# Two schemes for the same seven products become one: both halves of a feed-forward block chained in three PSUM accumulators, with a set's third product issued behind the next set's first

## The chip, the cores and the metric

The kernel runs on one core of a Trainium2 chip. The metric is device time in microseconds of one execution. The engines are named as in the profile: PE is TensorE (with PEld for its weight loads), DVE is VectorE, ACT is ScalarE, POOL is GpSimd, SP is SyncE, which here only issues DMAs.

## The reference, cut to what matters

A transformer block on x of 2048 x 576 in fp32: a conditioned layer norm, attention with a compressive memory, a second conditioned layer norm, and a SwiGLU feed-forward block of width 4608. The change is in the last part alone:

```python
def _B_ref(x, w_gate, w_up, w_down):
    g = _silu(x @ w_gate)
    u = x @ w_up
    return (g * u) @ w_down
...
h = _layernorm(x, axis=-1) * (1 + cb) + sb
x = x + gb * _B_ref(h, B_w_gate, B_w_up, B_w_down)
```

## The kernel before, in words

The first third of the span is attention and its output projection, with the layer norms. The rest is the feed-forward block, in two halves of 1024 tokens (t = 0 and 1). Each half runs over 18 pairs p of 128-column strips of the 4608 columns. For a pair, a gate set (z = 0) and an up set (z = 1) of products are computed, then the products with w_down of the pair before are added to the outputs.

Every set is a fast 2 x 2 block matrix product (Winograd's form of Strassen): seven products m = 1 to 7 instead of eight. Each product is one function call, `prod` (L1139): seven matmuls of 512 columns, since the operands are split in a high and a low part (wh and wl for weights, y for the activations) with the last rows, wr, packed into one matmul of their own. The four results of a set are, by the products' numbers and with U = 1 + 6, V = U + 7: (0,0) = 1 + 2, (0,1) = U + 5 + 3, (1,0) = V + 4 and (1,1) = V + 5. `fin` (L1154) finishes a result: Silu for the gate, the product with the gate's result for the up set.

The two halves compute these sums differently.

- First half, `step0` (L1178): each product has a PSUM bank of its own (tag M, four buffers). ScalarE copies product 1 to SBUF (L1184); VectorE adds every later product to a running sum in SBUF (L1189, L1192) or in `fin` (L1160, L1168).
- Second half, `step` (L1199): products 1, 6, 7 and 4 accumulate on each other in bank A (two buffers); ScalarE copies A out behind product 1 (into bank B, onto which product 2 then accumulates, L1212), behind product 6 (tb) and behind product 7 (tc, both L1174). Products 5 and 3 accumulate in bank C. VectorE adds only for (1,1) and (0,1). In its very first set bank B has not been written yet, and product 1 goes to SBUF (cu).

The order of the work is written out by hand. A pair has 14 steps k, one product each, in an order from a table: `MO0` (1, 2, 6, 7, 4, 5, 3) for both sets in the first half, with the two sets of its last pair interleaved (`ZML`); `MO7` (1, 5, 6, 2, 7, 4, 3) in the second, `MOB` for its first set. Around each product a step issues, by its number k, casts of weights PF or PF0 products ahead (`prep_w`, ScalarE, with the low part on VectorE one step later through the list `later`), loads of weights (`load_o`, SyncE), sums of weights for the fast product (`sum_o`, GpSimd; in the first half only, stored by `store_o` and `store_r` through ScalarE's DMA queue, and loaded again in the second), casts of the results (`prep_a`) and of w_down (`prep_d`). The down-products of the pair before follow the product of the step: in the first half `plain` (L1276, eight chunks of 12 matmuls with 288 columns, at steps 4 to 11), in the second `down` (L1261, a fast product again, 14 chunks of six matmuls, by the table `CH`; its operands are sums of the results, `sum_a` at steps `KS` and casts at `KA`). The last two pairs of the second half use `plain` as well, at the steps of `CH0`. Down-products have a PSUM tag of their own (dn, two buffers of two banks), and VectorE adds each chunk to an accumulator in SBUF.

While the first half runs, `prep2` (L996) prepares the second half's input piece by piece (a generator, advanced at steps 1 to 10): it loads rows of x, normalizes, stores, loads them back as xb, transposes on TensorE into an M bank, scales on ScalarE, and forms the seven activation operands on GpSimd, which are stored as yD. At the end of the first half `load_y` (L1067) loads them over the first half's y, each as soon as its last product has run.

```python
A: [1] -> copy to B -> [1+6] -> copy tb -> [1+6+7] -> copy tc -> [1+6+7+4]
B: copy of 1, then + 2            C: 5, read for (1,1), then + 3
```

## Time and profile before

| | before |
|---|---|
| median of three runs | 1987.38 us (1987.2 to 1988.35) |
| the profiled execution | 1991.21 us |
| its span, first to last instruction | 1989.4 us |
| granted TensorE clock, mean | 0.986 |
| TensorE / VectorE / ScalarE / GpSimd busy | 96% / 80% / 45% / 29% |
| first half of the feed-forward block, first product to first product of the second | 662.48 to 1351.13 us |

The span is cut into 40 slices of 49.7 us in the second part of the page; a digit is the busy share in tenths. Slices 14 to 27 are the first half of the block, the rest the second. A line of a group of instructions gives source line, engine, operation, output <- inputs, shapes and count, then busy us and mean ns, then the idle time of the engine just before them and what ended it. A line of waits gives who waited for whom, us in total, how often, and the longest. M, A, B, C and pd are PSUM tiles, sg, cu, tb and tc are SBUF tiles.

### The profile page before, as it was taken

What the parts mean: (1) busy time and instruction counts of PE and PEld (TensorE: products, weight loads), DVE (VectorE), ACT (ScalarE), POOL (GpSimd) and SP (SyncE); (2) the same over time, 40 slices, a digit from 0 to 9 for tenths busy, and PEclk for the clock granted to TensorE, in tenths of its full rate; (3) what the DMA queues carried; (4) which work ended last, traced back from release to release, by engine and by line L of the source; (5) the groups of instructions that cost most, each with busy time, mean ns of one, the idle gap of its engine ahead of it and who ended that gap; (6) DMA issues with size and microseconds to landing.
All of it is one profiled execution on the core that took longest, in us unless ns stands there. A gap on an engine that the chain in (4) does not pass through costs nothing.

```text
span 1989.4 us, 30854 instructions
## 1 busy us (share of the span) xinstructions
PE 1904.3 (96%) x10927; PEld 1573.1 (79%) x10927; DVE 1598.7 (80%) x3411; ACT 894.3 (45%) x1928; POOL 583.4 (29%) x772
## 2 busy tenths in 40 slices
PE   7999999999998799999999998989999999999998
PEld 5888856676766678878888877878888888888888
DVE  6575257878786899999899999876888888888886
ACT  2222257767666333344334334333454544454542
POOL 5212235555535544544454444310000000000000
PEclk9999999999999899999999999999999999999999
DMA  7767564445435544444444544367333333232341
GB/s 212 242 225 238 205 190 127 141 137 149 132 111 145 193 162 158 166 163 143 149 153 161 174 130 148 114 216 246 129 98 118 99 98 118 79 120 90 118 120 48
DMA packets 173545, 296.64 MB, mean 149 GB/s; under 512 B 25104, under 2 KB 101776, under 8 KB 171920
## 3 DMA queue, kind: packets, MB, share of 16 engines
q1 hardware_dynamic: 145504, 239.79, 38.5%
q10 hardware_dynamic: 27888, 54.89, 7.6%
q8 instruction: 86, 1.41, 0.3%
q14 instruction: 67, 0.55, 0.1%
HBM read 185.29 MB, written 109.31 MB: 148 GB/s over the span
## 4 chain that ended last, share of the span: by engine, by line
PE 65%; DVE 22%; DMA 5%; issue 3%; ACT 3%; POOL 1%; ACTq 0%; SPq 0%; DVEq 0%; POOLq 0%
PE A L1146 12%; PE pd L1269 9%; PE C L1146 6%; PE pd L1286 6%; PE M L1146 5%; DVE wl L1111 4%; PE s L590 4%; PE av L610 4%; PE pp L102 4%; PE s L188 4%; PE B L1146 3%; PE pv L102 3%; PE pw L708 2%; DVE sg L1169 2%; DVE acc L1290 2%
## 5 line engine op out<-in xcount | busy, mean ns | idle before, releaser
L1146 PE MATMUL M<-y,wh 128*128 128x512 f32 x1008 | 364.0, 402 | 22.1 <-DVE cu L1168 14.8
L193 DVE CUSTOM_DVE_ANT_0 junk<-s,tri 128x256 bf16<-128x256 f32 (+3 forms) x512 | 228.8, 487 | 78.7 <-PE s L188 71.4
L1111 DVE TENSOR_TENSOR wl<-O,wh 128x256 fp32r<-128x256 f32 x504 | 269.4, 535 | 14.4 <-ACT wh L1110 13.8
L1146 PEld LDWEIGHTS M<-y,wh 128*128 128x128 f32 x1008 | 193.7, 192 | 71.9 <-issue 20.9
L1229 ACT CAST ah<-sg 128x512 fp32r<-128x512 f32 x192 | 118.9, 619 | 291.4 <-DVE sg L1169 244.1
L1101 POOL TENSOR_TENSOR O<-O 128x384 f32<-128x384 f32 x144 | 164.8, 1158 | 229.3 <-DMA O<-in_wgu_dram 120.7
L593 ACT ACTIVATE Pt<-s 128x512 f32<-128x512 f32 (+1 forms) x352 | 187.1, 560 | 87.8 <-PE s L590 73.8
L1110 ACT CAST wh<-O 128x256 fp32r<-128x256 f32 x504 | 200.0, 404 | 16.2 <-issue 12.3
L1146 PE MATMUL A<-y,wh 128*128 128x512 f32 x576 | 202.5, 392 | 0.7 <-ACT cu L1174 0.7
L1146 PE MATMUL M<-y,wl 128*128 128x512 f32 x504 | 201.5, 400 | 0.0
L1286 PE MATMUL pd<-dh,ah 128*128 128x288 f32 x640 | 190.0, 297 | 2.3 <-DVE acc L1290 2.3
L1286 PE MATMUL pd<-dh,al 128*128 128x288 f32 x640 | 189.5, 296 | 1.4 <-DVE al L1230 1.4
L1286 PE MATMUL pd<-dl,ah 128*128 128x288 f32 x640 | 189.3, 296 | 0.0
L1274 DVE TENSOR_TENSOR acc<-acc,pd 128x576 f32<-128x576 f32 x216 | 159.5, 751 | 24.9 <-PE pd L1269 23.1
L1230 DVE TENSOR_TENSOR al<-sg,ah 128x512 fp32r<-128x512 f32 x192 | 141.8, 739 | 21.2 <-ACT ah L1229 21.2
L590 PE MATMUL s<-qs,ks 110*128 110x512 f32 (+2 forms) x384 | 151.3, 411 | 5.3 <-DMA qs<-mD 3.5
L1161 ACT ACTIVATE sg<-sg 128x512 f32<-128x512 f32 x109 | 69.2, 635 | 183.6 <-DVE sg L1160 183.5
L1290 DVE TENSOR_TENSOR acc<-acc,pd 128x576 f32<-128x576 f32 x156 | 116.6, 748 | 38.5 <-PE pd L1286 38.0
L188 PE MATMUL s<-ks,qs 108*128 108x256 f32 (+3 forms) x512 | 142.3, 329 | 2.8 <-DMA ks<-kD 1.4
L1269 PE MATMUL pd<-dh,ah 128*128 128x288 f32 x448 | 132.8, 296 | 0.0
L1269 PE MATMUL pd<-dh,al 128*128 128x288 f32 x448 | 132.6, 296 | 0.0
L1269 PE MATMUL pd<-dl,ah 128*128 128x288 f32 x448 | 132.5, 296 | 0.0
(367 smaller groups left out, 4617.2 us busy)
## 6 DMA issues: line engine op xcount, KB each, us to landing
O<-in_wgu_dram SPq DMA_DIRECT2D x36, 768.0 KB
oD<-O ACTq DMA_DIRECT2D x36, 512.0 KB
O<-oD SPq DMA_DIRECT2D x36, 512.0 KB
ks<-kD SPq DMA_DIRECT2D x68, 216.0 KB
qs<-qD SPq DMA_DIRECT2D x68, 216.0 KB
O<-in_wgu_dram SPq DMA_DIRECT2D x36, 384.0 KB
rD<-wr ACTq DMA_DIRECT2D x36, 336.0 KB
wr<-rD SPq DMA_DIRECT2D x36, 336.0 KB
```

The source lines that it names most:

```text
L188: nc.tensor.matmul(bank[:, n * (h - h0):n * (h - h0) + n], lhsT=qst[b][0:108, h, 128 * i:128 * i + 128], rhs=kst[b][0:108, h // 2, 0:n], s ...
L193: nc.vector.tensor_tensor_reduce(junk[:, :n], bank[:, n * (h - h0):n * (h - h0) + n], tri[:, L - n:], 1.0, -3e38, op0=ALU.add, op1=ALU.max ...
L590: nc.tensor.matmul(bank[:, n * (g - h):n * (g - h + w)].rearrange("p (a b) -> p a b", a=w), lhsT=kst[u % NB][0:110, g // 2, 128 * j:128 * ...
L593: nc.scalar.activation(pt[:, h:h + per, :n], bank[:, :n * per].rearrange("p (a b) -> p a b", a=per), AF.Exp, scale=SCALE)
L1101: nc.gpsimd.tensor_tensor(o[:, d], o[:, a], o[:, b], op=op)
L1110: nc.scalar.copy(wh, o)
L1111: later.append(lambda: nc.vector.tensor_tensor(wl, o, f32(wh), op=ALU.subtract))
L1146: nc.tensor.matmul(bank, lhsT=a, rhs=b, start=(first and n == 0), stop=(n == 6), skip_group_check=not first)
L1269: nc.tensor.matmul(pd[:, i, :288], lhsT=a[:, tk], rhs=w, start=(k == 0), stop=(k == 2))
L1274: nc.vector.tensor_tensor(o, o, pd[:, :, :288], op=ALU.add)
L1286: nc.tensor.matmul(pd[:, i, :288], lhsT=a[:, tk], rhs=w, start=(k == 0), stop=(k == 5))
L1290: nc.vector.tensor_tensor(o, o, pd[:, :, :288], op=ALU.add)
```

## The change

`step0` and its orders go; both halves use `step`, and one loop over t and p takes the place of two. The order of a set is 1, 6, 2, 7, 5, 4, and product 3 of a set is issued behind product 1 of the next set: step 1 computes product 3 of the previous pair's up set, step 8 that of the pair's own gate set. Step 1 of the very first pair has no product, and one product 3 is left for the end, before the last down-products. A third result comes later by that: `prep_a` of (1,1) is at step 13, of (1,0) at step 0 and, in the plain case, of (0,1) at step 2 of the next pair. To match, the down-products of the fast kind come in another order (`POS`), with their sums and casts later (`KS`, `KA`), and the plain ones at steps 2 to 5 and 7 to 10 in both halves. Weight casts run five products ahead throughout. The transposes of `prep2` go to a buffer of the tag dn instead of M. The reloads of y are issued at steps 7 and 9 to 13 of the first half's last pair and at step 1 of the second half.

```diff
-PF0 = 6
-CH0 = (0, 1, 1, 0, 1, 1, 0, 1, 0, 1, 1, 1, 0, 0)
+CH0 = (0, 0, 1, 1, 1, 1, 0, 1, 1, 1, 1, 0, 0, 0)
-KS = (0, 1, 2, 3)
-KA = ((5, 2), (6, 4), (7, 6), (3, 8))
+KS = (2, 3, 4, 5)
+KA = ((5, 3), (6, 5), (7, 7), (3, 8))
-WW = (19, 23, 25, 26, 27, 30)
+WW = (19, 23, 25, 27, 30)
-    POS = [1, 2, 4, 5, 6, 7, 3]
+    POS = [1, 4, 2, 5, 6, 7, 3]
...
+    MP = (1, 6, 2, 7, 5, 4, 3)
+    ZM = [(z if m != 3 else 1 - z, m) for z in range(2) for m in (1, 3, 6, 2, 7, 5, 4)]
...
-                    pt = ps.tile([P, 4, P], F32, tag="M", name="pt", bufs=4)
+                    pt = ps.tile([P, 2, L], F32, tag="dn", name="pt", bufs=2)[:, 0].rearrange("p (a b) -> p a b", b=P)
...
-    def step0(p, z, m):
-        bank = ps.tile([P, L], F32, tag="M", name=f"M{m}", bufs=4)
-        prod(z, m, bank, True, True)
...
         elif m == 7:
             copy_t("tc", bank)
-            fin(z, (1, 1), B["C"], T["tc"])
+        elif m == 5:
+            fin(z, (1, 1), bank, T["tc"])
...
+                    if k != 1 or prev is not None:
+                        step(z, m)
+                    if k == 1 and prev is not None:
+                        PA[0, 1] = AC[0, 1]
+                    if t == 0 and p == NPR - 1 and k in (7, 9, 10, 11, 12, 13) or t == 1 and p == 0 and k == 1:
                         load_y(ACT_OP[m])
-                    if k == 1:
-                        load_o(0, nx, 0)
-                    elif k == 8:
-                        load_o(0, nx, 1)
+                    if not last and k == 7 - PF:
+                        load_o(tn, nx, 0)
+                    elif not last and k == 14 - PF:
+                        load_o(tn, nx, 1)
...
-                elif not end and 9 <= k < 13:
-                    sum_o(nx, 1, k - 9)
+                        elif tn == 0 and k >= 11:
+                            sum_o(nx, 1, k - 11)
+                        elif k == 0 and p:
+                            sum_o(p, 1, 3)
...
-                elif k == 1:
-                    store_o(p, 1)
-                    store_r(p, 0)
+                        elif k == 2:
+                            store_o(p, 1)
+                        elif k == 5:
+                            store_r(p, 0)
...
-                for ij, kk, j in (((0, 0), 11, 1), ((1, 1), 12, 4), ((1, 0), 13, 2)):
+                    for ij, kk, j in (((0, 0), 11, 1), ((1, 1), 13, 4)):
...
         flush()
-        prep_a(prev[1] % 2, (0, 1), PA[0, 1])
+        step(1, 3)
+        prep_a(prev[1] % 2, (1, 0), PA[1, 0])
+        flush()
+        prep_a(prev[1] % 2, (0, 1), AC[0, 1])
```

More of the change, by code (lines that the diff above doesn't have):

```diff
@@ L895, in block @@
     NPR = NF // 2
-    MO0 = (1, 2, 6, 7, 4, 5, 3)
-    MO7 = (1, 5, 6, 2, 7, 4, 3)
-    MOB = (1, 6, 2, 5, 7, 4, 3)
-    ZM = [(z, m) for z in range(2) for m in MO0]
-    ZML = [(0, 1), (0, 2), (1, 1), (1, 2), (0, 6), (0, 7), (1, 6), (1, 7), (0, 4), (0, 5), (0, 3), (1, 5), (1, 4), (1, 3)]
-    ZM1 = [(z, m) for z in range(2) for m in MO7]
-    ZMB = [(0, m) for m in MOB] + [(1, m) for m in MO7]
-    def order(t, p):
-        if t == 0:
-            return ZML if p == NPR - 1 else ZM
-        return ZM1 if p else ZMB
+    MP = (1, 6, 2, 7, 5, 4, 3)
+    ZM = [(z if m != 3 else 1 - z, m) for z in range(2) for m in (1, 3, 6, 2, 7, 5, 4)]
     SLOT = {1: 0, 2: 1, 3: 6, 4: 2, 5: 4, 6: 5, 7: 3}
@@ L1137, in prep_d, with prod @@
         DP[p % 2, key] = (dh, dl)
-    def prod(z, m, bank, first, last):
+    def prod(z, m, bank, first):
         wh, wl = W.pop((z, m))
@@ L1176, in block @@
     B = {}
-    def step0(p, z, m):
-        bank = ps.tile([P, L], F32, tag="M", name=f"M{m}", bufs=4)
-        prod(z, m, bank, True, True)
-        end = p == NPR - 1
-        if m == 1:
-            T[z, 0] = tx.tile([P, L], F32, tag="tz", name="tz", bufs=1) if end and z else tmp("tb")
-            nc.scalar.copy(T[z, 0], bank)
-            return
-        u = T[z, 0]
-        if m == 7:
-            T[z, 1] = tx.tile([P, L], F32, tag="tw", name="tw", bufs=1) if end and z else tmp("tc")
-            nc.vector.tensor_tensor(T[z, 1], bank, u, op=ALU.add)
-            return
-        if m in (5, 6):
-            nc.vector.tensor_tensor(u, bank, u, op=ALU.add)
-        if m != 6:
-            ij = {2: (0, 0), 4: (1, 0), 5: (1, 1), 3: (0, 1)}[m]
-            fin(z, ij, bank, T[z, 1] if m in (4, 5) else u)
-            if z and not (end and m == 2):
-                prep_a(p % 2, ij, AC[ij])
     def step(z, m):
+        prime = "set" not in B
         if m == 1:
@@ L1205, in step @@
         bank = B["B" if m == 2 else "C" if m in (5, 3) else "A"]
-        prime = "set" not in B
-        prod(z, m, bank, m in (1, 5) or m == 2 and prime, m in (2, 4, 3))
+        prod(z, m, bank, m in (1, 5) or m == 2 and prime)
         if m == 1:
@@ L1212, in step @@
                 nc.scalar.copy(B["B"], bank)
+        elif m == 6:
+            copy_t("tb", bank)
         elif m == 2:
@@ L1215, in step @@
             B["set"] = True
-        elif m == 6:
-            copy_t("tb", bank)
         elif m == 7:
             copy_t("tc", bank)
-            fin(z, (1, 1), B["C"], T["tc"])
+        elif m == 5:
+            fin(z, (1, 1), bank, T["tc"])
         elif m == 4:
             fin(z, (1, 0), bank)
-        elif m == 3:
+        else:
             fin(z, (0, 1), bank, T["tb"])
@@ L1264, in down @@
         dh, dl = DP[p % 2, m]
-        pd = psd.tile([P, 2, L], F32, tag="dn", name="pd", bufs=2)
+        pd = ps.tile([P, 2, L], F32, tag="dn", name="pd", bufs=2)
         for i in range(2):
@@ L1277, in plain @@
         b, h, c = c // 4, c // 2 % 2, c % 2
-        pd = psd.tile([P, 2, L], F32, tag="dn", name="pd", bufs=2)
+        pd = ps.tile([P, 2, L], F32, tag="dn", name="pd", bufs=2)
         for i in range(2):
@@ L1355, in block @@
         load_o(0, 0, 1)
-        gt, gw = chain(tr[1], tr[2]), iter(MO0[:PF0])
+        gt, gw = chain(tr[1], tr[2]), iter(MP[:PF])
         for i in range(4):
@@ L1389, in block @@
         ap_ = pool(p4, "ap", 4)
-        psd = pool(p4, "psd", 1, space=PSUM)
+        ps = pool(p4, "ps4", 1, space=PSUM)
         p6 = ExitStack()
         x2p = pool(p6, "x2p")
-        tx = pool(p6, "tx")
-        ps = pool(p6, "psm", 1, space=PSUM)
         g2 = prep2()
@@ L1398, in block @@
         new_acc(accp, (2, 3, 4, 5))
-        seq = [(t, p, z, m) for t in range(2) for p in range(NPR) for z, m in order(t, p)]
+        seq = [(p, z, m) for t in range(2) for p in range(NPR) for z in range(2) for m in MP]
+        late = {}
         prev = None
-        n, nw = 0, PF0
-        def ahead(pf):
-            nonlocal nw
-            while nw < len(seq) and nw <= n + pf:
-                prep_w(*seq[nw][1:])
-                nw += 1
-        load_d(0, 0)
-        for p in range(NPR):
-            nx = (p + 1) % NPR
-            end = p == NPR - 1
-            if end:
-                run(g2)
-            for k in range(14):
-                z, m = order(0, p)[k]
-                todo, later[:] = later[:], []
-                ahead(PF if end and k > 6 else PF0)
-                n += 1
-                for f in todo:
-                    f()
-                step0(p, z, m)
-                if end:
-                    if z:
-                        load_y(ACT_OP[m])
-                    if k == 0:
-                        prep_r(0, p, 1)
-                    elif k == 7:
-                        load_o(1, 0, 0)
-                    elif k == 8:
-                        load_o(1, 0, 1)
-                        prep_a(p % 2, (0, 0), AC[0, 0])
-                    elif k == 11:
-                        prep_r(1, 0, 0)
-                else:
-                    if k == 1:
-                        load_o(0, nx, 0)
-                    elif k == 8:
-                        load_o(0, nx, 1)
-                    if k == 3:
-                        prep_r(0, p, 1)
-                    elif k == 9:
-                        prep_r(0, nx, 0)
-                if k in (1, 2):
-                    mul_d(p, k - 1)
-                elif k in (3, 4, 8, 7) and p < NPR - 2:
-                    sum_d(p, (3, 4, 8, 7).index(k))
-                if not end and 4 <= k < 8:
-                    sum_o(nx, 0, k - 4)
-                elif not end and 9 <= k < 13:
-                    sum_o(nx, 1, k - 9)
-                if k in (4, 5, 6, 10):
-                    j = (4, 5, 6, 10).index(k)
-                    prep_d(p, (j // 2, j % 2), j)
-                if k == 0 and p == 0:
-                    store_o(p, 0)
-                elif k == 1:
-                    store_o(p, 1)
-                    store_r(p, 0)
-                elif k == 7:
-                    store_r(p, 1)
-                elif k == 10:
-                    nc.scalar.dma_start(wdD[p][:, :NS[p]], RW[p][:, :NS[p]])
-                elif k == 11 and not end:
-                    store_o(nx, 0)
-                elif k == 12 and not end:
-                    load_d(0, nx)
-                if prev is not None and DS <= k < DS + 8:
-                    plain(*prev, k - DS)
-                if p == 0 and (0, k) in RS:
-                    load_res(0, RS[0, k])
-                if k in G2 and p > 0:
-                    next(g2, None)
-            prev = (0, p)
@@ L1475, in block @@
-        p6.close()
-        accq = pool(p4, "acq")
-        new_acc(accq, (1, 6, 7))
-        ps = pool(p4, "ps4", 1, space=PSUM)
-        late = {}
-        for p in range(NPR):
-            last = p == NPR - 1
-            nx = p + 1
-            if last:
-                load_x11(1)
-            chunk = 0
-            for k in range(14):
-                z, m = order(1, p)[k]
-                todo, later[:] = later[:], []
-                ahead(PF)
-                n += 1
-                for f in todo:
-                    f()
-                step(z, m)
-                if not last and k == 7 - PF:
-                    load_o(1, nx, 0)
-                if not last and k == 14 - PF:
-                    load_o(1, nx, 1)
-                if k == 2:
-                    prep_r(1, p, 1)
-                if not last and k == 9:
-                    prep_r(1, nx, 0)
-                if is_plain(*prev):
-                    if k == 0 and prev[0]:
-                        prep_a(prev[1] % 2, (0, 1), PA[0, 1])
-                    if CH0[k]:
-                        f = plain(*prev, chunk)
-                        if f:
-                            late[k + 3] = f
-                        chunk += 1
-                    if k in late:
-                        late.pop(k)()
-                else:
-                    for j in range(4):
-                        if k == KS[j]:
-                            sum_a(j)
-                    for j, kk in KA:
-                        if k == kk:
-                            prep_a(prev[1] % 2, j, PA[ASRC[j]])
-                    for _ in range(CH[k]):
-                        down(*prev, chunk)
-                        chunk += 1
-                if last and 1 <= k < 9:
-                    comb(k - 1)
-                if p == 0 and (1, k) in RS:
-                    load_res(1, RS[1, k])
-                if k == 2:
-                    load_d(1, p)
-                if is_plain(1, p):
-                    if k in (4, 5, 6, 10):
-                        j = (4, 5, 6, 10).index(k)
-                        prep_d(p, (j // 2, j % 2), j)
-                elif k >= 7:
-                    prep_d(p, POS[k - 7], WSLOT[POS[k - 7]])
-                for ij, kk, j in (((0, 0), 11, 1), ((1, 1), 12, 4), ((1, 0), 13, 2)):
-                    if k == kk:
-                        prep_a(p % 2, ij if is_plain(1, p) else j, AC[ij])
-            for f in late.values():
-                f()
-            late.clear()
-            PA.clear()
-            PA.update(AC)
-            prev = (1, p)
@@ new lines, in block, with due @@
+        n, nw = 0, PF
+        def due(k):
+            if k in late:
+                late.pop(k)()
+        load_d(0, 0)
+        for t in range(2):
+            for p in range(NPR):
+                last = t == 1 and p == NPR - 1
+                nx = (p + 1) % NPR
+                tn = t if nx else t + 1
+                if t == 0 and p == NPR - 1:
+                    run(g2)
+                    p6.close()
+                    accq = pool(p4, "acq")
+                    new_acc(accq, (1, 6, 7))
+                if last:
+                    load_x11(1)
+                chunk = 0
+                for k in range(14):
+                    z, m = ZM[k]
+                    todo, later[:] = later[:], []
+                    while nw < len(seq) and nw <= n + PF:
+                        prep_w(*seq[nw])
+                        nw += 1
+                    n += 1
+                    for f in todo:
+                        f()
+                    if k != 1 or prev is not None:
[3 more added lines that the diff above has]
+                    if t == 0 and p == NPR - 1 and k in (7, 9, 10, 11, 12, 13) or t == 1 and p == 0 and k == 1:
+                        load_y(ACT_OP[m])
+                    if not last and k == 7 - PF:
+                        load_o(tn, nx, 0)
+                    elif not last and k == 14 - PF:
+                        load_o(tn, nx, 1)
+                    if k == (2 if t else 3):
+                        prep_r(t, p, 1)
+                    elif not last and k == 9:
+                        prep_r(tn, nx, 0)
+                    if t == 0:
+                        if k in (1, 2):
+                            mul_d(p, k - 1)
+                        elif k in (3, 4, 8, 7) and p < NPR - 2:
+                            sum_d(p, (3, 4, 8, 7).index(k))
+                        if tn == 0 and 4 <= k < 8:
+                            sum_o(nx, 0, k - 4)
+                        elif tn == 0 and k >= 11:
+                            sum_o(nx, 1, k - 11)
+                        elif k == 0 and p:
+                            sum_o(p, 1, 3)
+                        if k == 0 and p == 0:
+                            store_o(p, 0)
+                        elif k == 2:
+                            store_o(p, 1)
+                        elif k == 5:
+                            store_r(p, 0)
+                        elif k == 7:
+                            store_r(p, 1)
+                        elif k == 10:
+                            nc.scalar.dma_start(wdD[p][:, :NS[p]], RW[p][:, :NS[p]])
+                        elif k == 11 and tn == 0:
+                            store_o(nx, 0)
+                        elif k == 12 and tn == 0:
+                            load_d(0, nx)
+                    elif k == 2:
+                        load_d(1, p)
+                    if prev is not None and is_plain(*prev):
+                        if k in (0, 2):
+                            ij = (1, 0) if k == 0 else (0, 1)
+                            prep_a(prev[1] % 2, ij, PA[ij])
+                        if CH0[k]:
+                            f = plain(*prev, chunk)
+                            if f:
+                                late[k + 3] = f
+                            chunk += 1
+                        due(k)
+                    elif prev is not None:
+                        for j in range(4):
+                            if k == KS[j]:
+                                sum_a(j)
+                        if k == 0:
+                            prep_a(prev[1] % 2, 2, PA[1, 0])
+                        for j, kk in KA:
+                            if k == kk:
+                                prep_a(prev[1] % 2, j, PA[ASRC[j]])
+                        for _ in range(CH[k]):
+                            down(*prev, chunk)
+                            chunk += 1
+                    if last and 1 <= k < 9:
+                        comb(k - 1)
+                    if p == 0 and (t, k) in RS:
+                        load_res(t, RS[t, k])
+                    if is_plain(t, p):
+                        if k in (4, 5, 6, 10):
+                            j = (4, 5, 6, 10).index(k)
+                            prep_d(p, (j // 2, j % 2), j)
+                    elif k >= 7:
+                        prep_d(p, POS[k - 7], WSLOT[POS[k - 7]])
+                    for ij, kk, j in (((0, 0), 11, 1), ((1, 1), 13, 4)):
+                        if k == kk:
+                            prep_a(p % 2, ij if is_plain(t, p) else j, AC[ij])
+                    if t == 0 and k in G2 and p > 0:
+                        next(g2, None)
+                for k in sorted(late):
+                    due(k)
+                PA.clear()
+                PA.update(AC)
+                prev = (t, p)
@@ L1543, in block @@
         flush()
-        prep_a(prev[1] % 2, (0, 1), PA[0, 1])
+        step(1, 3)
+        prep_a(prev[1] % 2, (1, 0), PA[1, 0])
+        flush()
+        prep_a(prev[1] % 2, (0, 1), AC[0, 1])
         for c in range(8):
```

## The prediction

> **What bounds the kernel now.** I read the page's first two parts, then the busy time by stage, then TensorE's waits in the two halves of the feed-forward block, which are all that the change touches.

> ```profile
> span 1989.4 us, 30854 instructions
> PE 1904.3 (96%) x10927; PEld 1573.1 (79%) x10927; DVE 1598.7 (80%) x3411; ACT 894.3 (45%) x1928; POOL 583.4 (29%) x772
> PE   7999999999998799999999998989999999999998
> DVE  6575257878786899999899999876888888888886
> ```

> TensorE is the bound nearly everywhere; the second line of slices shows VectorE (DVE) full as well in slices 14 to 25. Busy time in three stretches (each engine's figure is us, with its instruction count behind it; then granted clock, DMA share, GB/s): the first pair of the first half, its other 17 pairs, the second half.

> ```profile
> 662.50:697.50 35.00, 30.98 (x127) 23.81 (x126) 28.57 (x44) 14.85 (x32) 17.37 (x15) 0.97 0.76 250
> 697.50:1351.10 653.60, 620.36 (x3320) 535.24 (x3319) 594.61 (x911) 248.37 (x559) 281.09 (x251) 0.98 0.48 158
> 1351.10:1960.00 608.90, 606.31 (x3241) 527.68 (x3240) 506.50 (x936) 287.43 (x664) 0.00 (x0) 1.00 0.36 113
> ```

> The second half already runs TensorE 99.6% of the time (606.31 of 608.90). The first has 95%, with VectorE at 91%. TensorE's waits in the first half, then in the second:

> ```profile
> PE M L1146 <- DVE cu L1168: 14.8, 13, 2.0
> PE pt L1048 <- DMA xb<-xh: 6.6, 3, 3.9
> PE M L1146 <- ACT tb L1184: 6.0, 12, 1.6
> PE M L1146 <- DVE wr L1096: 5.3, 1, 5.3
> PE pd L1286 <- DVE acc L1290: 2.3, 5, 0.6
> ...
> PE A L1146 <- DMA wr<-rD: 1.9, 1, 1.9
> PE pd L1286 <- DVE al L1230: 1.4, 1, 1.4
> PE A L1146 <- ACT cu L1174: 0.7, 1, 0.7
> ```

> A product waits until VectorE has drained the bank of four products earlier. What these waits really cost needs TensorE's floor. Two pieces of the chain of waits give it (start, length): a product followed by a plain down-product takes 3.22 us, the product alone 1.62, and a pair of the second half 34.11.

> ```profile
> 1325.51 1.62 PE M L1146 x7
> ...
> 1328.72 1.62 PE M L1146 x7
> ...
> 1426.02 1.84 PE C L1146 x7
> ...
> 1460.13 1.83 PE C L1146 x7
> ```

> A pair of the first half has 14 products and 8 down-products: 6 x 1.62 + 8 x 3.22 = 35.5 us; 17 of them are 603, pair 0 without down-products 22.7, and the 12 groups of transposes about 3. Floor: 629 us. The timeline has the first product at 662.48 and the second half's first at 1351.13: 688.7 us. So the first half loses 58 to 60 us (58 when summed over late starts). 37 us are named waits in full list; 11 are matmuls at 0.43 us instead of 0.23 after some of them; the rest is the restart around each wait.

> The trace lets the clock go early: behind the wait of 1.79 us at 735.8 about ten matmuls start 0.43 us apart, 2 us lost, while behind the 1.05 us at 774.1 none do. [...]

> **The change part by part.**

> *VectorE is relieved.* A set of seven products (one weight matrix of a pair) now costs VectorE 7 instructions for the gate and 11 for the up matrix: every product is an add or fused into one. In the chain it is 2 and 6. That is 10 fewer per pair, 180 in all, at 0.68 to 0.735 us by these rows:

> ```profile
> L1192 DVE TENSOR_TENSOR tb<-M,tb 128x512 f32<-128x512 f32 x70 | 47.9, 684 | 5.3 <-PE M L1146 5.3
> L1168 DVE TENSOR_TENSOR cu<-M,tc 128x512 f32<-128x512 f32 x34 | 23.1, 680 | 0.0
> L1184 ACT COPY tb<-M 128x512 f32<-128x512 f32 x35 | 20.3, 580 | 14.8 <-PE M L1146 14.8
> L1174 ACT COPY tc<-A 128x512 f32<-128x512 f32 x35 | 20.6, 590 | 82.6 <-PE A L1146 82.6
> ```

> 180 x 0.69 = 124 us off VectorE's 623 in the first half: 499 of some 640, 78%, below the second half's 83%, at which TensorE waits almost nowhere. The matmuls are the same in number and kind, and 1.62 us per product in both halves, so only waits can go.

> *ScalarE gets more.* Three copies per set instead of one: 72 x 0.58 = 42 us more on 263, 305 of 640, 48%, as in the second half (287 of 609, 47%).

> *New waits.* Products 6, 7 and 4 accumulate in a bank that ScalarE has to have copied first. Uncovered, such a copy costs 0.95 us: in the second half's first set product 6 follows at once, and starts 1.18 us after the last matmul of product 1 where 0.23 is due. With another product (1.62 us) between, there is 1.62 - 0.95 = 0.7 us to spare. In the changed order each of the three has one between: the previous set's product 3, then 2, then 5, and mostly a down-product too. Between: 0 (the second half after its first set, 53 pairs of such copies and products, shows none) and 0.95 x 108 = 103 us. I take 0, since the nearest row is the second half, and 1 us for pair 0, where nothing is behind product 1.

> *Banks C and B* wait for VectorE, with three products or more in between (product 5 of a set is read long before the late product 3 adds to it; at least two steps, 3.2 us, against two adds of 0.69). 0.

> *Pair 0* has no down-products, steps of 1.62 us and a full ScalarE: 14 x 0.40 casts, 6 x 0.58, 4 x 0.63, 4 x 0.62, 4 x 0.43, 2 x 0.94, plus five DMA issues of about 0.5, 20 us of 21. It loses 9.6 us now (32.3 between its first copy and the next pair's, floor 22.7). Between 1 and 9; I take 4.

> *Transposes of the second half's input* move from the four M banks to the two of the down-products. 12 times one of the two is taken, so that the next down-product needs the previous one drained. Bounds 0 and 12 x 0.6 (the longest wait on acc) = 7; I take 2, as 1.9 us pass before and VectorE is less full.

> *Their loads.* The 6.6 us on xb (with slow matmuls 10.5) arise at 971.8 and 1241.1: SyncE issued the 768 KB load of weights at 963.05 and 1232.99 and the xb loads right behind, in steps without down-products. The weight load moves one step later (behind xb) and the down-products begin two steps earlier, so the three steps' notice grows from 5 to 8 us and more. Left: 0 to 10.5; I take 2.

> *The end of the first half.* Now the last pair interleaves its sets, so that y can be reloaded early, and pays 5.3 us plus 3 slow (clock 0.57) for the rest rows wr at 1317. In order, wr is due seven products later: gone. But the reloads of y (7 x 1.2 MB) are issued from step 7 on instead of step 2. At the 340 GB/s of 1342 to 1370 (summed per us from the DMA records), y, two weight loads and wr, some 9.5 MB, need 28 us, and the products ask for them within 32 after 2 us of latency. Between -2.6 (the 1.9 and 0.7 of the second half's start go) and +8; I take 4 in place of 2.6.

> *SyncE, ScalarE's and GpSimd's queues.* Weight loads (one step later), store_o and store_r (one and four later) and the fourth sum of z = 1 (to the next pair) each keep three steps or more; GpSimd sits idle for 117 us on these loads now and keeps its count. ScalarE's issue of store_o behind the late sum could hold its copies: priced below. 2 us.

> *Second half.* The same instructions, product 3 one product later, sums and casts of the operands one or two steps later with their down-products reordered to match. It has 2.6 us of waits in 609, so nothing to gain; per pair 0 to 0.5, I take 0.1, 1.5 in all.

> *The end.* Now product 3 covers operand (1,0) and still 1.4 us remain on al L1230; afterwards product 3 is again last. 0.

> *Before the block* one weight cast less (0.40 and 0.65 us): 0.

> Sum: 58 - (4 + 2 + 2 + 2) - (4 - 2.6) - 1.5 = 45 us. The profiled run took 1991.21 (span 1989.4 and 1.8 around it), 0.2% above the median of 1987.38; taken off that median: 1942.4 us.

> **The rivals.**

> *Half the gain.* What ends last is not VectorE but loads: xb stays at 10, y's reload stalls 8, shared banks 7, pair 0 stays at 9. For it: DMA share 0.76 in pair 0 and 0.93 around 1316 to 1324. Against it: 0.48 over the half, and the waits on DVE are over half of the named ones. 58 - 34 + 2 = 26 less a little: 1963 us.

> *ScalarE late: slower.* ScalarE now waits 124 us for VectorE at the Silu alone (L1161, behind sg L1160) and more at the casts ah; were its copies to come late behind these and behind DMA issues that wait for GpSimd, TensorE would wait at the places with only one product and no down-product between: product 7 to 4 of the up set and 1 to 6 of the gate set, 2 x 18. The 0.7 us to spare used up, each 1.3 us beyond eats the gain: from 2.0 us of lateness at all 36 the kernel is slower. At 3 us: 36 x 2.3 = 83 - 45 = 38 slower, 2025. Against it: those waits on VectorE come from its backlog, which goes. [...]

> *The second half loses what the first gains.* At 99.6% any new wait shows. If the late product 3 makes each pair wait for operand 5 or bank C by one cast and one add (0.62 + 0.69, plus restart), 2 us x 18 = 36: 1942 + 36 = 1978, faster by little or the same with more. For it: VectorE at 83% in order. Against: at least three steps (7 us) lie between product 3 and the down-product that needs it.

> **How the numbers follow.** Forecast 0.78, half the gain 0.09, the second half losing it 0.06, ScalarE late 0.07. Own range of the forecast 1934 to 1955 (all leftovers gone: 58 - 1 - 2; or pair 0, xb and y at two thirds). 0.2%, 4 us, is what can be told from no change. Faster: 0.78 + 0.09 + 0.03 = 0.90; same 0.03; slower 0.07. Range 1932 to 1966: down to all 58 gone, up through half the gain.

> **What would show it.** The first half from its first product to the second half's first falls from 688.7 to about 640; its VectorE busy to about 500; no M rows; the waits on cu and tb gone; the clock there at 1.00. Half the gain: pt <- xb and A <- y or wr rows of several us. ScalarE late: A <- ACT tb, tc or B rows, 30 or more times. Second half: its 608.9 us over 615. I am wrong if VectorE's waits go and the first half does not shorten by at least 35.

## The result: 0.3% faster where 2.3% was forecast

| | before | after |
|---|---|---|
| median of ten runs each, on one chip | 1988.62 us (1987.01 to 1992.88) | 1984.21 us (1979.0 to 1985.18) |
| ratio after / before | | 0.997, 95% interval 0.9959 to 0.9981 |
| profiled execution, span | 1991.21, 1989.4 us | 1984.63, 1982.9 us |
| first half, first product to first product of the second | 688.7 us | 677.2 us |
| second half, from there to the end of the span | 638.3 us | 643.0 us |

The forecast was 1942.4 us, between 1932 and 1966. In the profiles the first half gives 11.5 us where some 48 were expected (688.7 to about 640), and the second takes 4.7 back; the difference, 6.8, is that of the spans (6.5) but for where the first product starts. Of both figures 1.6 us are one product: the first half's last product 3 now runs behind the boundary.

From the first two parts of the page of the changed kernel:

```profile
span 1982.9 us, 30559 instructions
PE 1893.6 (95%) x10927; PEld 1572.5 (79%) x10927; DVE 1519.2 (77%) x3231; ACT 925.8 (47%) x2000; POOL 580.9 (29%) x772
DVE  6575257878786887877788788764888888888886
```

The full slices 14 to 25 of VectorE are gone, by the first line of engines: 180 instructions fewer, 79.5 us less. Yet TensorE is no better used. Busy time of the two halves of the block (columns as in the prediction: TensorE, weight loads, VectorE, ScalarE, GpSimd; then clock, DMA share, GB/s):

```profile
662.70:1339.90 677.20, 642.04 (x3438) 557.64 (x3438) 540.70 (x775) 298.69 (x662) 296.17 (x265) 0.99 0.50 160
1339.90:1960.00 620.10, 612.46 (x3290) 535.88 (x3289) 514.09 (x943) 285.43 (x666) 0.00 (x0) 0.99 0.37 117
```

VectorE is 80% busy in the first half, ScalarE 44%, and TensorE stands for 35 us. TensorE's waits in the block say for what (rows of the attention part left out; al and ah are the low and the high part of a result that a down-product reads, wr the rest rows of a weight):

```profile
PE pd L1254 <- DVE al L1198: 31.7, 18, 2.2
...
PE A L1134 <- DMA wr<-rD: 7.5, 2, 6.2
...
PE pd L1254 <- ACT ah L1197: 1.8, 1, 1.8
...
PE A L1134 <- ACT tb L1162: 1.1, 1, 1.1
PE A L1134 <- ACT B L1179: 0.8, 3, 0.3
PE A L1134 <- ACT cu L1162: 0.7, 1, 0.7
PE C L1134 <- DVE cu L1156: 0.4, 1, 0.4
...
PE A L1134 <- ACT wh L1098: 0.2, 1, 0.2
```

Every wait that the change was to remove is gone: cu (14.8), tb (6.0), the late wr at 1317 (5.3), xb (6.6), acc (2.3). In their place stands one row, the first. It is the same matmul in every pair: the first plain down-product of the pair before, now at step 2, waits for the low part (al) of operand (1,0), which VectorE has not yet formed. One of the 18 is the known 1.4 us at the end of the kernel; the other 17, 30.3 us, are in the first half. One such place, on TensorE, from the timeline (start, length):

```profile
844.28 0.29 PE L1254 MATMUL pd<-dl,ah 128*128 128x288 f32 x1
846.40 0.40 PE L1254 MATMUL pd<-dh,al 128*128 128x288 f32 x1 [1.82 <-DVE al L1198]
```

VectorE and GpSimd over the same microseconds (wl is the low part of a weight; dr is w_down, ha a piece of the second half's input):

```profile
840.78 0.69 DVE L1153 TENSOR_TENSOR sg<-A,sg 128x512 f32<-128x512 f32 x1
841.38 1.06 DVE L1099 TENSOR_TENSOR wl<-O,wh 128x256 fp32r<-128x256 f32 x1
842.37 1.92 DVE L1198 TENSOR_TENSOR al<-sg,ah 128x512 fp32r<-128x512 f32 x1
844.20 0.95 DVE L1099 TENSOR_TENSOR wl<-O,wh 128x256 fp32r<-128x256 f32 x1
845.07 1.27 DVE L1198 TENSOR_TENSOR al<-sg,ah 128x512 fp32r<-128x512 f32 x1
```

```profile
840.73 3.00 POOL L1112 TENSOR_TENSOR dr__10500<-dr__10500,gbB 128x576 f32<-128x576 f32 x2 [2.08 <-DMA dr__10500<-in_wd_dram]
843.70 1.17 POOL L1048 TENSOR_TENSOR ha<-ha 128x256 f32<-128x256 f32 x1
844.83 2.18 POOL L1117 TENSOR_TENSOR dr__10500<-dr__10500 128x288 f32<-128x288 f32 x2
```

ScalarE is not late here: its cast ah of (1,0) ran from 841.91 to 842.52, 2.5 us before the al that needs it began. (In one pair it is: the row of 1.8 us on ah stands at 1306, just ahead of that pair's wait on al.) VectorE is late, with four instructions in a row that read two operands from SBUF. Run alone, wl takes 0.42 us and al 0.68 (their shortest times in this profile); here, with GpSimd at work beside them, 1.06, 1.92, 0.95 and 1.27. The four are 3.0 us longer than that, and the stall is 1.82. The multiplication just ahead of them, sg<-A,sg, with one operand in PSUM, takes its usual 0.69 beside the same GpSimd instruction.

The same in the sums, VectorE's groups by shape in the first half, of before and of after (count | busy us, mean ns):

```profile
L1230 DVE TENSOR_TENSOR al<-sg,ah 128x512 fp32r<-128x512 f32 x70 | 57.9, 827 | 5.3 <-ACT ah L1229 5.3
```

```profile
L1198 DVE TENSOR_TENSOR al<-sg,ah 128x512 fp32r<-128x512 f32 x69 | 82.6, 1197 | 3.3 <-ACT ah L1197 3.3
...
L1153 DVE TENSOR_TENSOR sg<-B,sg 128x512 f32<-128x512 f32 x18 | 12.5, 692 | 1.1 <-PE B L1134 0.5
L1148 DVE TENSOR_TENSOR sg<-C,tb 128x512 f32<-128x512 f32 x18 | 12.4, 690 | 6.0 <-PE C L1134 6.0
```

Before, 15 of 70 al were longer than 0.75 us; after, 40 of 69. Al alone is 25 us more. The records of the two engines tie each long one to GpSimd: all 55 began while a GpSimd instruction was running and ended 0.55 us behind the end of one, and of the 84 others none began beside one. By operand, al of (1,0), for which TensorE waits, is long in 16 of 17 pairs, and in none before. No instruction with an operand in PSUM is longer than 0.69 us (0.76 for the wider acc) in the first half of either kernel. So the theory to test: the gain went into one new wait, made by two things together, a down-product too soon behind its operand, and GpSimd's work on w_down beside VectorE's instructions on two SBUF operands. Rivals: VectorE's order or load alone makes it; or ScalarE; or the end of the first half.

The second half's loss, beside the product that it took over, goes with the other row, wr<-rD: the longer of its two waits is 6.2 us at 1367, for rest rows that SyncE asked for only at 1353.83, behind the reloads of y and the next weights.

### The profile page after: what moved, and what is told of

The parts are those of the page before. It is cut to its first block, busy times and chain, and to the rows that moved or that the text cites. A ratio compares the mean times of both kernels' runs of the same rounds, so it can differ in the third digit from the quotient of the medians.

```text
span 1982.9 us, 30559 instructions
## 1 busy us (share of the span) xinstructions
PE 1893.6 (95%) x10927; PEld 1572.5 (79%) x10927; DVE 1519.2 (77%) x3231; ACT 925.8 (47%) x2000; POOL 580.9 (29%) x772
## 4 chain that ended last, share of the span: by engine, by line
PE 78%; DVE 13%; DMA 5%; issue 1%; ACT 1%; POOL 1%; SPq 0%; ACTq 0%; DVEq 0%; POOLq 0%
PE A L1134 17%; PE pd L1254 12%; PE pd L1237 9%; PE C L1134 9%; PE B L1134 5%; PE pp L101 4%; PE s L589 4%; PE av L609 4%; DVE wl L1099 4%; PE s L187 4%; DVE al L1198 3%; PE pv L101 3%; PE pw L707 2%; DVE dl L1124 1%; DMA mD<-mr 1%
## 5 line engine op out<-in xcount | busy, mean ns | idle before, releaser
L1134 PE MATMUL A<-y,wh 128*128 128x512 f32 x1152 | 407.0, 394 | 2.9 <-ACT tb L1162 1.1
L1134 PEld LDWEIGHTS A<-y,wh 128*128 128x128 f32 x1152 | 217.0, 188 | 49.4 <-ACT B L1179 3.8
L1134 PE MATMUL A<-y,wl 128*128 128x512 f32 x576 | 227.0, 394 | 0.0
L1134 PE MATMUL C<-y,wh 128*128 128x512 f32 x576 | 202.7, 392 | 0.4 <-DVE cu L1156 0.4
L1254 PE MATMUL pd<-dl,ah 128*128 128x288 f32 x640 | 189.9, 297 | 0.0
L1198 DVE TENSOR_TENSOR al<-sg,ah 128x512 fp32r<-128x512 f32 x192 | 166.9, 869 | 12.2 <-ACT ah L1197 12.2
L1254 PEld LDWEIGHTS pd<-dh,al 128*128 128x128 f32 x640 | 121.6, 190 | 35.9 <-DVE al L1198 35.9
L1149 ACT ACTIVATE sg<-sg 128x512 f32<-128x512 f32 x73 | 46.2, 633 | 204.4 <-DVE sg L1148 204.3
```

The costliest lines, as they stand in the source:

```text
L1134: nc.tensor.matmul(bank, lhsT=a, rhs=b, start=(first and n == 0), stop=(n == 6), skip_group_check=not first)
L1198: later.append(lambda: nc.vector.tensor_tensor(al, src, f32(ah), op=ALU.subtract))
L1254: nc.tensor.matmul(pd[:, i, :288], lhsT=a[:, tk], rhs=w, start=(k == 0), stop=(k == 5))
```

## The experiments

Runs of one group share a chip and the runs of the kernel before on it, so ratios are compared, not times across groups. Diffs are against the changed kernel, if nothing else is said. The waits shown are TensorE's in the feed-forward block.

### Is it the place of the down-products?

`start3` begins the plain down-products at step 3 instead of 2, `start4` at step 4, as the kernel before did (the two added lines, in this order).

```diff
-CH0 = (0, 0, 1, 1, 1, 1, 0, 1, 1, 1, 1, 0, 0, 0)
+CH0 = (0, 0, 0, 1, 1, 1, 1, 1, 1, 1, 1, 0, 0, 0)
+CH0 = (0, 0, 0, 0, 1, 1, 1, 1, 1, 1, 1, 1, 0, 0)
```

> One line of the changed kernel: the eight plain down-products stand at steps 3 to 10 instead of 2 to 5 and 7 to 10, so the first comes one product (1.62 us) later. Theory A (the first down-product of a pair waits about 2 us for the low part al of operand (1,0), which VectorE reaches late after four steps without down-products): the waits on al fall from 18 of 1.8 us to about 0.3 us each, the slow clock behind them goes too, and the kernel gains 30 to 38 us on the changed one: 1946 to 1954. Theory B (VectorE is late throughout the first half, and any order only moves the wait): waits on acc, cu or al of the same total appear elsewhere, and the gain is under 10 us.

> The same, with the down-products at steps 4 to 11, where the kernel before has them. Theory A: no wait on al is left in the first half, 35 to 42 us off the changed kernel, 1942 to 1949; a little better than the start at step 3, since there VectorE ends al about 0.3 us after it is asked for. Theory B: as above, under 10 us.

Before on this chip: 1982.97 us, median of seven. `start3`: 1955.65 us, ratio 0.9859 (0.984 to 0.9877). `start4`: 1965.45, ratio 0.9911 (0.9891 to 0.993). Their waits, first `start3`, then `start4`:

```profile
PE pd L1254 <- DVE al L1198: 6.8, 11, 1.4
PE A L1134 <- DMA wr<-rD: 5.2, 2, 4.0
PE A L1134 <- ACT B L1179: 4.9, 4, 4.1
```

```profile
PE A L1134 <- ACT tb L1162: 21.2, 16, 2.4
...
PE A L1134 <- DMA wr<-rD: 4.3, 1, 4.3
```

The changed kernel stands at 0.9991 on this chip (measured with a later group), so one step later is worth 1.3%: the place of the first down-product is a cause. The waits on al fell about as expected, the time by 26 us where 30 to 38 were; the row on B is new. Two steps later should have taken the rest away, and did take all of al (only the 1.4 us at the end is left); but `start4` is slower than `start3`, since another wait appears in 16 pairs: ScalarE's copy tb. It had been there all along, under the down-products. ScalarE in `start4` (in brackets what it waited for):

```profile
876.08 0.58 ACT L1162 COPY tb<-A 128x512 f32<-128x512 f32 x1 [3.19 <-DVE cu L1156]
```

The buffer tb is single. The late sum for (0,1), cu<-C,tb, still reads the old tb, and VectorE comes to it only at 875.29, behind wl and al of 1.06, 1.28 and 1.02 us; until then ScalarE cannot write the next tb, nor TensorE add product 7. In the changed kernel ScalarE waits the same way, while TensorE is at the down-products of steps 2 and 3 and in the wait on al among them:

```profile
ACT tb L1162 <- DVE cu L1156: 65.7, 17, 4.6
```

`start3` also shows one long stretch, in VectorE's and GpSimd's records:

```profile
1272.67 4.21 DVE L1157 TENSOR_TENSOR sg<-cu,sg 128x512 f32<-128x512 f32 x1
```

```profile
1272.60 1.01 POOL L1089 TENSOR_TENSOR O<-O 128x384 f32<-128x384 f32 x1
1273.57 2.77 POOL L1112 TENSOR_TENSOR dr__15131<-dr__15131,gbB 128x576 f32<-128x576 f32 x2
```

A multiplication of 0.69 us begins 0.07 us behind the first of GpSimd's three instructions and lasts until 0.55 us behind the last, and ScalarE and then TensorE stand behind it (the 4.1 us on B).

### Is it VectorE's order?

`alfirst` turns the list of what VectorE has to do at step 1, so that al of (1,0) comes before the wl.

```diff
                     todo, later[:] = later[:], []
...
+                    if k == 1:
+                        todo.reverse()
```

> The changed kernel with only the order of two VectorE instructions turned at step 1: al of operand (1,0) before the low part of a weight, wl (0.95 us in the pair read). Theory A: each of the 18 waits falls from about 1.8 to 0.9 us and several slow-clock stretches go: 15 to 25 us off, 1960 to 1969. Theory B: nothing, within 5 us.

One run: 1959.12 us, ratio to the median of before 0.988. The al wait is 14.5 us in 14 places, about half. So one wl of 1 us in front of it was half of the lateness, and the order counts; but it does not remove the wait.

### Is it GpSimd?

`nopool` leaves out GpSimd's scaling and sums of w_down (its results' places are filled by two more loads).

```diff
+            if p < NPR - 2:
+                nc.sync.dma_start(r[:, 4:6].rearrange("p a b -> p (a b)"), wd[2 * p])
+                nc.sync.dma_start(r[:, 6], wd[2 * p][:, 0:288])
...
-        nc.gpsimd.tensor_tensor(v, v, gbB, op=ALU.mult)
+        pass
...
-        nc.gpsimd.tensor_tensor(r[:, d], r[:, a], r[:, b], op=ALU.subtract)
+        pass
```

> The changed kernel without GpSimd's work on w_down (its scaling by the gate and the four differences are left out; the three slots of the differences are filled by two more DMAs instead, so that the stored size stays). Theory A1 (VectorE is late there because GpSimd runs beside it: al took 1.92 and 1.27 us and wl 1.06 and 0.95 in the pair read, against 0.69 and 0.42 in the second half, where GpSimd is idle): al falls to a mean of 0.7 us at that place, the 18 waits to under 0.5 us each, and 30 to 40 us go. Theory A2 (VectorE is late by its queue alone): durations and waits stay, under 8 us go.

One run: 1941.22 us, ratio 0.979. Its waits, and al among VectorE's groups in the first half:

```profile
PE A L1137 <- DMA wr<-rD: 7.9, 2, 6.4
...
PE pd L1257 <- DVE al L1201: 2.0, 2, 1.4
```

```profile
L1201 DVE TENSOR_TENSOR al<-sg,ah 128x512 fp32r<-128x512 f32 x70 | 55.7, 795 | 2.7 <-ACT ah L1200 2.7
```

With the down-products where the change put them, and VectorE's order as it is, the wait disappears with GpSimd's share: al is back at 55.7 us, and the first half takes 636.4 us, within what the prediction gave it (about 640). Both things are needed for the wait; taking away either removes it.

The counterpart, `before_nopool`, is the kernel before without the same GpSimd work (the diff is the same, in that kernel).

> The kernel before, without GpSimd's work on w_down (scaling and differences left out, three slots filled by two more DMAs). It asks how much of the kernel before's own loss came from GpSimd beside VectorE, and so whether the chain was needed at all. If VectorE's load alone bounds it there (22 us of named waits on cu, tb and acc): under 15 us faster than before. If GpSimd makes VectorE late there too: its instructions with two SBUF operands shorten (wl 0.66 us, al 0.83, dl 0.74 to about 0.55, 0.70, 0.55), some 35 us of VectorE's time, most of the waits on it go and the kernel is 25 to 40 us faster.

One run, on another chip: 1957.14 us against 1984.66 (nine runs), ratio 0.986. What is left of the waits of its first half:

```profile
PE pt L1048 <- DMA xb<-xh: 7.8, 2, 5.0
PE M L1149 <- DVE wr L1096: 4.3, 1, 4.3
...
PE M L1149 <- DVE cu L1171: 3.5, 5, 2.0
```

The cu row falls from 14.8 to 3.5 and no al is longer than 0.69 us. So much of what the kernel before lost, and what the prediction put down to 180 instructions too many, was GpSimd beside VectorE as well: about 1.4%, against 2.0% of the changed kernel (0.9991 on that chip, next group, to 0.979).

### Can the operand come later, and the rest rows sooner?

`changed` is the changed kernel again, beside the others of this group. `defer11` moves cast and al of operand (1,1), which is needed last, from step 13 to step 3 of the next pair, so that less stands ahead of (1,0). `defer_wr`, on top of it, loads the rest rows of the second half's first up set at step 1, ahead of the reload of y.

```diff
                         if k in (0, 2):
                             ij = (1, 0) if k == 0 else (0, 1)
                             prep_a(prev[1] % 2, ij, PA[ij])
+                        if k == 3:
+                            prep_a(prev[1] % 2, (1, 1), PA[1, 1])
...
-                        if k == kk:
+                        if k == kk and not (ij == (1, 1) and is_plain(t, p)):
...
+        prep_a(prev[1] % 2, (1, 1), PA[1, 1])
```

The last line stands at the end of the kernel, ahead of the last down-products. What `defer_wr` adds:

```diff
+                    if t == 1 and p == 0 and k == 1:
+                        prep_r(1, 0, 1)
...
-                    if k == (2 if t else 3):
+                    if k == (2 if t else 3) and (t, p) != (1, 0):
```

> The changed kernel itself, beside the kernel before on the chip of the following runs, as their base. On the chip of the result it stood at 0.997 of the kernel before; every theory expects 0.995 to 0.999 here.

> The changed kernel with one cast moved: in the first half (and before the last plain down-products) the cast and low part of operand (1,1), which only the fifth down-product of a pair needs, are issued at step 3 of the next pair instead of step 13. Theory A (VectorE's queue at the steps without down-products makes al of (1,0) late): the instruction of 1.9 us ahead of it goes, it ends about when it is asked for, the waits on al in the first half fall from 31 us to under 6, and 28 to 38 us go. Theory B (some other instruction of VectorE takes its place): waits of the same size stay, under 10 us.

> As defer11, and the load of the packed rows of the up set in the second half's first pair is issued one step earlier, ahead of the last reload of y and of the next weights. Theory: the wait of 6 us on that load (wr, at 1367 us in the changed kernel) falls to under 1 us, y comes at most 1 us late: 4 to 7 us below defer11. Rival: the 3 us of DMA that it passes arrive later by as much, and a wait on y of the same size takes its place: within 2 us.

Before on this chip: 1984.0 us, 13 runs. `changed`: 1981.34, ratio 0.9991 (0.998 to 1.0003): here the change can't be told from none. `defer11`: 1955.19, ratio 0.9861 (0.9844 to 0.9879); al still waits 12.7 us in 14 places where under 6 was expected (and 26 us are gained on the changed kernel where 28 to 38 were); the al waited for is long, 1.22 to 1.92 us, in 12 of the 13 places of the first half, so the operand that remains meets GpSimd too. `defer_wr`: 1948.63, ratio 0.9822 (0.9801 to 0.9842), and its row for the load is

```profile
PE A L1134 <- DMA wr<-rD: 0.9, 1, 0.9
```

against 6.7 in `defer11`: the place of that load in SyncE's queue is what the second half lost, and 6.6 us is its price.

### Is it the single buffer tb?

`start4_tb2` is `start4` with two buffers for tb; to make room for it, the tag of the gate results has six instead of seven. `start4_nsg6` is `start4` with only the second edit.

```diff
-NSG = 7
+NSG = 6
...
-            t1, t2, t3, t4 = [tp.tile([P, L], F32, tag=g, name=g, bufs=2 if g == "cu" else 1) for g in ("tb", "tc", "cu", "cu")]
+            t1, t2, t3, t4 = [tp.tile([P, L], F32, tag=g, name=g, bufs=1 if g == "tc" else 2) for g in ("tb", "tc", "cu", "cu")]
...
-        T[tag] = t = tmp(tag, 2 if tag == "cu" else 1)
+        T[tag] = t = tmp(tag, 1 if tag == "tc" else 2)
```

> As start4, with two buffers for the copy tb (and six instead of seven for the results, to make room). In start4 16 waits of 1.3 us on the copy tb took the place of those on al. Theory C (the copy waits for VectorE to have read the previous set's tb, in the late sum for (0,1), and step 2 to 4 have no down-product to cover it): with two buffers these waits go, 20 to 28 us below start4, 1937 to 1945 on that chip. Rival: ScalarE itself is late by its casts, and they stay, within 5 us.

> The control for start4_tb2: start4 with six buffers of the results and the one of tb. Theory C (the single buffer of tb made the 16 waits): they stay at 18 to 24 us, time within 6 us of start4's 1965. Rival (the number of result buffers did it): the waits go, and the time falls to about 1940.

`start4_tb2`, in the group of `changed`: 1939.16 us, one run, ratio 0.977, and no wait on tb. `start4_nsg6`, on the other chip: 1967.9, one run, ratio 0.992, with the wait unchanged:

```profile
PE A L1134 <- ACT tb L1162: 21.7, 16, 2.4
```

So the second buffer, and not the other tag's size, is worth `start4`'s remaining 1.4%.

### All together

`best` is `start4_tb2` with the early load of `defer_wr`.

> start4_tb2 (down-products at steps 4 to 11, two buffers of tb, six of the results) with the early load of the packed rows of defer_wr. Theory: the waits on al and tb are gone and the one on wr with them, some 12 us of TensorE's waits are left in the block; ratio to the kernel before 0.974 to 0.978, about 1932 to 1940. Rival (the gains overlap, since the reload of y would end last instead): 0.978 or above.

1937.89 us (1936.77 to 1941.15) against 1984.66, ratio 0.9764 (0.975 to 0.9777): faster than both kernels. The stretch from 660 to 1290 (its first half runs from 662.27 to 1297.85), al there, and TensorE's three largest waits in the block:

```profile
660.00:1290.00 630.00, 625.41 (x3405) 547.19 (x3405) 528.68 (x770) 293.91 (x658) 290.62 (x265) 1.00 0.52 169
```

```profile
L1198 DVE TENSOR_TENSOR al<-sg,ah 128x512 fp32r<-128x512 f32 x68 | 74.4, 1094 | 0.1
```

```profile
PE A L1134 <- DMA y<-yD: 2.7, 2, 1.4
...
PE pd L1237 <- DVE acc L1242: 1.7, 2, 1.2
PE pd L1254 <- DVE al L1198: 1.4, 1, 1.4
```

TensorE is 99.3% busy (625.41 of 630.00) and the first half takes 635.6 us. GpSimd still works beside VectorE, al is still 1.09 us instead of 0.68; but nothing now asks for a result before it is there.

## Why the prediction was right in its parts and wrong in its sum

**Right.** The floor: 629 us plus 10 of leftovers for the first half were reached, at 636.4 (`nopool`) and 635.6 (`best`), of which 1.6 are the product that moved to the second half. The loss of 58 us was there to be had: `best` is 47 us faster than before on its chip, against 45 in the sum. The waits named went, those on cu and tb, the late wr, the loads of xb (no row of several us left). The added copies cost 2.6 us in named waits, 1.1 + 0.8 + 0.7 (the last was there before), of the 103 that were the upper bound; 0 plus 1 for pair 0 was taken. ScalarE: 298.7 us, 305 predicted. Pair 0, the transposes on the shared banks and the end of the kernel gave no row beyond what was allowed. The 9.6 us that pair 0 was said to lose were read between copies of ScalarE, the second of which ran late: by TensorE's first products pair 0 took 24.9 us before, 2.2 over its floor, and the rest was lost in the pairs behind it.

**Wrong: the step "VectorE is relieved", in its last sentence**, that the matmuls are the same and "so only waits can go". The working priced each wait that the change takes away and each copy that it adds, but of the operands' casts, which the change moves later, only those of the second half (0.1 us a pair). The plain case of the first half got no line. It was in the diff: casts at steps 13, 0 and 2, down-products from step 2 on. Counted out, steps 11, 12, 13, 0 and 1 have no down-product and last 1.62 us each; between the cast of (1,0), at step 0, and its use in the second group of matmuls at step 2 lie one step and a product. Before, the same operand was cast at step 11 and first used at step 4 of the next pair: six steps and a product. The rival on the second half had a mechanism of this kind, a pair waiting for an operand at about 2 us, 36 in all; but it named another operand, the one behind the late product 3, and the other half, and the distance that spoke against it there was not counted for the first half. Measured: 17 times 1.8 us, 30.3 in all, and in four of the 17 the clock's half rate behind.

**Wrong: VectorE's durations.** 499 us of VectorE in the first half were predicted, by 180 times 0.69 off 623; 540.7 were measured. The removed instructions are of the kind that was stretched nowhere in either first half (an operand in PSUM, 0.69 us at the most); those that stay are partly of the kind that was (al up to 1.91 us before, 2.57 after), and the change moves al of (1,0) beside GpSimd's work on w_down (long in 16 of 17 pairs, in none before), and al of (1,1) from beside the differences of w_down to beside its scaling (1.19 us in the mean before, 1.64 after). The profile of before showed that kind in its means, al 827 ns in the first half where its shortest are 0.68 us. The 78% for VectorE was compared with the second half's 83%, in which GpSimd does nothing at all (0.00 in its column of the window); as a cover it was not the same thing. `nopool` shows that this decides: without that GpSimd work VectorE is busy for 484 us in the first half, and the step comes out as predicted.

The records of the traces say of the two engines this much. In the pair shown al took up to 1.92 us where 0.68 is its shortest, and sg<-A,sg, with an operand in PSUM, took 0.69 at the most in all 17 of its places in that half. Every long al began while a GpSimd instruction was running and ended 0.55 us behind the end of one, and so did the instruction of 4.21 us in `start3`, through three of them. What in the two engines stretches the one beside the other, no run shows.

**Mis-sized: "the end of the first half".** 4 us were taken in place of 2.6, with an upper end of +8. The wait for the rest rows alone is 7.5 us. The mechanism was named (y's reloads fill the queue), the place too; `defer_wr` confirms it with 6.6 us. The rate of 340 GB/s was too good for its stretch: the trace of before has 284 in the mean from 1342 to 1370. The 2 us of latency are what that trace shows with little else on the queues (77 GB/s from 972.4 to 975.8): the loads of xb issued at 972.49 and 973.57 landed 2.2 and 2.1 us later. And the changed kernel, which does reach 315 to 385 from 1335 on, asks for the reloads late, each behind the last product that reads the old y. The clock was to be 1.00 in the first half and is 0.99, from the half rate behind some of the new waits.

**What hid it all.** A second wait, of ScalarE on the single tb (65.7 us in the changed kernel), costs nothing as long as down-products cover it, and 21 us when they begin at step 4. The prediction's test of the copies asked only whether ScalarE has the time, not whether the buffer that it writes is free.

What stays open: how much of the kernel before's loss is VectorE stretched beside GpSimd and how much the count of instructions. Without GpSimd's work on w_down the two kernels stand at 0.979 and 0.986 of before, so there the change is worth about 0.7%; but these are one run each, on two chips, and a version with GpSimd's work and without VectorE's extra 180 adds in the old order was not made.

## What to carry to other kernels

When a change moves the making of an operand later, or its use earlier, count for each use the steps and microseconds between the two, in the order in which the engine that makes it really gets to it; a sum of removed waits says nothing on that. Take an instruction's duration from the stretch in which it will run: where a group's mean is well above its shortest and GpSimd is busy, look for instructions on two SBUF operands that are stretched (al: 1.20 us in the mean, 0.68 the shortest); here 124 us of instructions on PSUM were taken away, and VectorE's busy time in the first half fell by 82. After removing a wait, look for the next single buffer behind it before moving the work that covers it.

## What the runs showed of the hardware that was not expected

- An elementwise VectorE instruction of 0.69 us took 4.21 us beside GpSimd (`start3`), with no row of waits on VectorE to tell of it: it counts as busy time. The sign is the end: 0.55 us behind the end of a GpSimd instruction, in all 55 long al of the two kernels' first halves.
- Behind a stall of TensorE the granted clock falls in some cases and not in others of the same length. After 2.23 us at 922.96 about eleven matmuls start at half rate, after 2.17 us at 884.17 none do. The windows of the changed kernel (last three columns: clock, DMA share, GB/s):

```profile
924.00:926.50 2.50, 2.50 (x9) 2.12 (x8) 2.25 (x6) 1.13 (x3) 0.00 (x0) 0.50 0.67 208
884.00:888.00 4.00, 3.83 (x24) 3.53 (x25) 3.35 (x7) 2.72 (x6) 0.00 (x0) 1.00 0.55 153
```
